# Listing a tile's row maximum and exponential one tile earlier, with a fifth head pair loaded unsplit

## The chip, the cores and the metric

The kernel runs on one core of a Trainium2 chip: TensorE for matrix products and transposes, VectorE, ScalarE and GpSimd for the rest, and DMA queues fed by SyncE. The metric is the device time of one execution in microseconds (us), the median of several. In the profile PE is TensorE (PEld its weight loads), DVE is VectorE, ACT ScalarE, POOL GpSimd, SPq the DMA issues of SyncE.

## What is computed

Attention with a threshold, then a two-layer network, all in float32:

```python
# q, k, v: 8 batches, 8 heads, 576 positions, 64 wide
scores = scale * q @ k.T
thresh = max(scores, -1) - tau
scores = where(scores >= thresh, scores, -1e9)
attn = exp(scores - max(scores, -1))
x = (attn / (sum(attn, -1) + 1e-9)) @ v        # heads side by side: 4608 x 512
h = x @ w_in                                   # 512 x 2048
out = (h * tanh(softplus(h))) @ w_out          # 2048 x 512
```

## The kernel before

Two heads of a batch make a head pair; there are 32 pairs. The 1152 rows of a pair's scores are cut into 9 tiles of 128 rows, so that attention is 288 tiles, and a loop over `g` (line 767) walks through them. Each pass, a step, does one stage of several tiles: scores of tile g+1, the softmax work of g and g-1, the transposes of g-2, the copies of the transposes of g-3, and the products with v some steps later. Batches of the first matrix product (`gemm1`) begin in step 42 and are then fed between the tiles, 14 matmuls in most steps (`advance`, line 858). After the tiles comes the second product.

Every engine but SyncE runs its instructions in the order in which the Python code lists them (class `InOrder`, line 62). So the order of the calls in a step is the order of each engine's queue, and an instruction that waits holds up all behind it on its engine.

The work on one tile:

- `scores` (line 386) multiplies q and k into one of two PSUM buffers `s` (pool `pss`, two buffers of two banks). Pairs 0 to 3 are *plain*: q and k are loaded as float32, and each product is made from the two halves of the array's rows. From pair 4 on each operand is split into a high and a low part after loading, by a ScalarE cast and a GpSimd subtraction for each of its eight pieces (`q_part`, `k_part`).
- `row_max` (line 409), VectorE: the negated maximum of a row of scores, into a small tile `st` (three buffers).
- `exponential` (line 416): the maximum scaled, on ScalarE for tiles below `COLUMNS` and on VectorE from there; the threshold on VectorE; the exponential of the scores on ScalarE, into `e` (two buffers).
- `masked` (line 425): one VectorE instruction compares the scores with the threshold, multiplies by the exponential and adds up each row. It is the last reader of the scores' buffer.
- `total` (line 432): one small instruction that adds 1e-9 to the sum, on ScalarE below `COLUMNS`, on VectorE from there. `normalise` (line 438): a reciprocal on VectorE and a multiplication on GpSimd.
- `transposes` (line 446) on TensorE into `tp` (one buffer); `evacuate` (line 464) copies that out on ScalarE: one copy for an even tile of a pair, two for an odd one, four for the ninth.
- `values` (line 483): a pair's product with v, in two times five pieces that `multiply` takes from a list.

Besides, the steps up to about 57 decode the weights `w_in`, 16 chunks of them. A chunk begun in step n has its `first` (two ScalarE instructions) in step n+3, `clamp` and `shift` (VectorE) in n+4 and n+5, `join` in n+6 (its `sign` on VectorE, its `add` on GpSimd), the cast `upper` (ScalarE) in n+8, and the subtraction `lower` in n+8 on GpSimd or, for the chunks in `ONV`, in n+9 on VectorE. Chunks begin where g mod 18 is 1, 5, 8, 12 or 15.

VectorE's order in a step before the change: row maximum of g, threshold of g, reciprocal of g-1, clamp, shift or lower, sign, mask of g. ScalarE's: copies of tile g-3, total of g-1, scaling of g, exponential of g, `first`, then whatever else the step has. In steps 2 to 37 TensorE has scores of g+1, transposes of g-2 and up to two value pieces; from step 38 (`SOON`) on the transposes come last in the step, and up to five pieces are taken.

Of the kernel before, what the change touches and what calls it, by code (L numbers as in the profile page):

```python
# [16 lines left out]
NP = H // 2  # L17
LOADS = ((0, 0, 2, 4, 5, 4, 7, 6, 7, 8), (0, 3, 3, 2, 5, 4, 5, 8, 8, 9), (0, 1, 2, 6, 3, 4, 7, 5, 7, 8))
# [5 lines left out]
PIECES = 2  # L24
WARM = (24, (26, 12, 6, 4, 3, 2, 2, 2, 2, 2))
SOON = 9 * NP + 2
# [18 lines left out]
SEVEN = range(2, B - 2)  # L45
BEGIN = {42: 0, 78: 1, 9 * 29: B - 2, **{36 * b + 45: b for b in SEVEN}}
MAKE = (66, 5)
COLUMNS = 45
FROM, TO = 36 * SEVEN[0] + 45, 9 * 29
AHEAD = (110, 112, 114)  # L50
XBUFS, TBUFS = 10, 8
# [6 lines left out]
def fv(ap):  # L58
    return ap.bitcast(F32)
# [78 lines left out]
def attention_moe(tc, q, k, v, tau, w_in, w_out, out):  # L138
    nc = tc.nc
    from contextlib import ExitStack  # L140

    with ExitStack() as outer:
# [9 lines left out]
        ident = cst.tile([P, P], F32, name="ident")  # L152
# [97 lines left out]
        nc = Engines(tc)  # L250
        with ExitStack() as first:
# [6 lines left out]
            with ExitStack() as att:  # L258
# [71 lines left out]
                    )  # L330

                def prep(pi):
                    plain = pi < NP
                    qs, k1, k2 = [], [], []
                    for a in range(2):
                        kind = F32 if plain else F32R
                        qs.append(ops.tile([P, 640], kind, name=f"q{a}"))
                        k1.append(ops.tile([P, S + D], kind, name=f"k1{a}"))
                        k2.append(None if plain else ops.tile([P, S + D], kind, name=f"k2{a}"))
                    made = dict(qs=qs, k1=k1, k2=k2, plain=plain)  # L340
                    made["vf"] = ops.tile([P, 2, 5, D], F32, name="vf")

                    def part(src, n):
                        r = raw.tile([P, 320], F32, name="r")
                        nc.sync.dma_start(r[:, :n], src)
                        return r[:, :n]

                    def q_part(c):
                        a, half = divmod(c, 2)
                        sl = slice(half * 320, (half + 1) * 320)  # L350
                        at = slice(c * 320, (c + 1) * 320)
                        if plain:
                            nc.sync.dma_start(qs[a][:, sl], q[pi, :, at])
                            return skip
                        r = part(q[pi, :, at], 320)

                        def split():
                            nc.scalar.copy(qs[a][:, sl], r)
                            nc.gpsimd.tensor_tensor(qs[a][D:, sl], r[D:], fv(qs[a][D:, sl]), ALU.subtract)

                        return split

                    def k_part(a, c):
                        sl = slice(c * 320, (c + 1) * 320)
                        if plain:
                            rows = slice(c * D, (c + 1) * D)
                            nc.sync.dma_start(k1[a][rows, :HB + D], k[pi, rows, a, c * HB:c * HB + HB + D])
                            return skip
                        r = part(k[pi, :, a, sl], 320)

                        def split():
                            nc.scalar.copy(k1[a][:, sl], r)
                            nc.gpsimd.tensor_tensor(k2[a][:, sl], r, fv(k1[a][:, sl]), ALU.subtract)

                        return split

                    def v_part(a):
                        nc.sync.dma_start(made["vf"][:, a], v[pi, :, a])
                        return skip

                    loads = [lambda c=c: q_part(c) for c in range(4)]
                    loads += [lambda a=a, c=c: k_part(a, c) for a in range(2) for c in range(2)]
                    loads += [lambda a=a: v_part(a) for a in range(2)]
                    return made, loads
# [24 lines left out]
                def row_max(s):  # L409
                    st = sm.tile([P, 8], F32, name="st")  # L410
                    e = sm.tile([P, 2, HB], F32, name="e", bufs=2)
                    nm = st[:, 0:1]
                    nc.vector.tensor_reduce(nm, s[:, :, :HB], AX.XY, ALU.max, negate=True)
                    return st, e

                def exponential(g, s, st, e):
                    nm = st[:, 0:1]
                    if g < COLUMNS:
                        nc.scalar.activation(st[:, 2:3], nm, AF.Copy, scale=SCALE)
                    else:  # L420
                        nc.vector.tensor_scalar(st[:, 2:3], nm, SCALE, None, ALU.mult)
                    nc.vector.tensor_scalar(st[:, 1:2], nm, -1.0, back, ALU.mult, ALU.subtract)
                    nc.scalar.activation(e, s[:, :, :HB], AF.Exp, bias=st[:, 2:3], scale=SCALE)
# [8 lines left out]
                def total(g, st):  # L432
                    if g < COLUMNS:
                        nc.scalar.activation(st[:, 4:5], st[:, 3:4], AF.Copy, bias=1e-9)
                    else:
                        nc.vector.tensor_scalar(st[:, 4:5], st[:, 3:4], 1e-9, None, ALU.add)
# [6 lines left out]
                def odd(g):  # L443
                    return g % 9 % 2

                def transposes(g):

                    both = tiles[g]["both"]
                    at = odd(g) * (S + D)
                    tp = pst.tile([P, 4, P], F32, name="tp")  # L450
                    for c in range(4):
                        nc.tensor.transpose(tp[:, c, :], both[:, at + c * P:at + (c + 1) * P], ident)
                    t5 = None
                    last = g % 9 == 8
                    if odd(g) or last:
                        t5 = pst.tile([P, 512], F32, name="t5")[:, :P]
                        if last:
                            nc.tensor.transpose(t5, both[:, S - P:S], ident)
                            nc.tensor.transpose(t5[:D], both[:, S - D:S], ident)
                        else:  # L460
                            nc.tensor.transpose(t5, both[:, 4 * P:5 * P], ident)
                    return tp, t5
# [241 lines left out]
                NT = NPAIRS * 9  # L704
                clock = [0]
# [4 lines left out]
                tiles = {}  # L710
# [7 lines left out]
                def start_pair(g, pi):  # L718
                    parts, todo = prep(pi)
                    pairs[pi] = dict(ops=parts, pt={})  # L720
                    for work, step in zip(todo, LOADS[0 if pi == 1 else 1 if 2 <= pi < NP else 2]):
                        loads.setdefault(g + step, []).append(work)

                def begin(g):
# [12 lines left out]
                def multiply(n):  # L737
                    for _ in range(n):
                        if pieces:
                            work, then = pieces.pop(0)  # L740
                            work()
                            if then:
                                ready.append(then)
# [13 lines left out]
                warm_up(WARM[0])  # L757
                pairs[0] = dict(pt={})
                pairs[0]["ops"], todo = prep(0)
                splits = [todo[i]() for i in FIRST[:3]]  # L760
                nc.sync.dma_start(back, tau)
# [5 lines left out]
                for g in range(NT + 6):  # L767
# [24 lines left out]
                        tiles[g - 2]["tp"] = transposes(g - 2)  # L792
                    done, ready[:] = ready[:], []
                    if not seven:
                        multiply(5 if g >= SOON else PIECES)
                    if g >= NT:
                        done += ready
                        ready.clear()
                    if g < NT:
                        tiles[g]["st"], tiles[g]["e"] = row_max(tiles[g]["s"])  # L800
                    if 1 <= g <= NT:
                        total(g - 1, tiles[g - 1]["st"])
                    if g < NT:
                        exponential(g, tiles[g]["s"], tiles[g]["st"], tiles[g]["e"])
                    for work in now:
                        if len(work) == 2:
# [28 lines left out]
                        chores.setdefault(max(g + 2, 2), []).append(work())  # L835
                    if weights and g % 18 in W1_STEPS:
                        decoding.append([()] * LAG + weights.pop(0)())
                    if g < NT:
                        if g < JOIN:
                            for work in now:  # L840
                                if len(work) == 3:
                                    work[2]()
                        if not odd(g):
                            both = sm.tile([P, S if g % 9 == 8 else 2 * S], F32, name="p" if g % 9 < 8 else "p8", bufs=2 if g % 9 < 8 else 1)
                        tiles[g]["both"] = both
                        half = both[:, S:] if odd(g) else both[:, :S]
                        tiles[g]["p"] = masked(g, tiles[g]["s"], tiles[g]["st"], tiles[g]["e"], half)
# [200 lines left out]
```

## Time and profile before

| | before |
|---|---|
| median of 3 runs | 1313.31 us (1312.69 to 1315.34) |
| profiled execution | 1313.38 us, its span 1311.6 us |
| busy, share of the span | TensorE 97%, VectorE 74%, ScalarE 65%, GpSimd 59% |
| mean granted clock of TensorE | 0.995 |

The span runs from the first to the last instruction of the profiled execution. TensorE's matmuls overlap one another and their ends are modelled, so that its busy time is not time at its peak. The granted clock is the share of 2.4 GHz that the chip gives TensorE; it has two levels, 1.0 (2.4 GHz) and 0.5 (1.2 GHz), and a value between is a mean over a stretch.

### The profile page before, as it was taken

How to read it: one execution, taken by the hardware profiler on the slowest of the kernel's cores; microseconds unless marked ns; L12 is line 12 of the kernel's file. 1: busy time of each engine (PE TensorE's matmuls, PEld its weight loads, DVE VectorE, ACT ScalarE, POOL GpSimd, SP SyncE). 2: the span in 40 equal slices, each digit the busy share in tenths (PEclk: the TensorE clock that was granted, in tenths of full speed). 3: DMA queues.
4: the chain of work that ended last, by engine and by line, in shares of the span. 5: the costliest groups of instructions: out<-in, count | busy, mean ns of one | idle time of the engine just before them, and what ended most of it. 6: DMA issues, size and time to landing. Idle time of an engine off the chain costs nothing. (4 is left out here: it accounts for less than half of the span.)

```text
span 1311.6 us, 28496 instructions
## 1 busy us (share of the span) xinstructions
PE 1272.1 (97%) x9749; PEld 1142.2 (87%) x9749; DVE 969.6 (74%) x2502; ACT 852.9 (65%) x1678; POOL 777.6 (59%) x1073
## 2 busy tenths in 40 slices
PE   8877999999999999999999999999999999999998
PEld 6435899899888888889888898989889999999998
DVE  6887877777778887888888785537985766667664
ACT  5887877777766666676676666664755554555552
POOL 3788887878776686686677676523303333444431
PEclk9998999999999999999999999999999999999999
DMA  6444555777556656566655654215735444344440
GB/s 185 129 128 124 154 160 149 206 215 235 161 162 189 194 163 204 163 184 196 194 169 176 212 157 142 73 50 166 243 116 158 129 134 141 113 145 134 141 130 32
DMA packets 169825, 205.16 MB, mean 156 GB/s; under 512 B 28880, under 2 KB 142544, under 8 KB 165584
## 3 DMA queue, kind: packets, MB, share of 16 engines
q1 hardware_dynamic: 169680, 203.34, 50.9%
q8 instruction: 77, 1.26, 0.4%
q14 instruction: 68, 0.56, 0.1%
HBM read 143.52 MB, written 59.77 MB: 155 GB/s over the span
## 5 line engine op out<-in xcount | busy, mean ns | idle before, releaser
L72 DVE SCALAR_TENSOR_TENSOR p<-s,st,e 128x576 f32<-128x576 f32 x288 | 234.6, 815 | 130.4 <-ACT e L72 128.6
L72 POOL TENSOR_SCALAR p<-p,st 128x576 f32<-128x576 f32 x288 | 243.8, 847 | 98.0 <-DVE st L72 71.9
L72 POOL TENSOR_TENSOR z<-z 128x256 f32<-128x256 f32 x128 | 124.5, 977 | 222.9 <-DVE z L72 214.1
L72 PE MATMUL s<-k,q 128*128 128x288 f32 (+1 forms) x1280 | 232.3, 326 | 19.2 <-DVE p L72 19.0
L72 ACT ACTIVATE e<-s,st 128x576 f32<-128x576 f32 x288 | 215.7, 749 | 42.9 <-DVE st L72 39.8
L72 DVE TENSOR_REDUCE st<-s 128x1 f32<-128x576 f32 x288 | 217.0, 753 | 22.2 <-PE s L72 22.0
L72 DVE TENSOR_TENSOR gl<-z,gh 128x1792 fp32r<-128x1792 f32 (+1 forms) x72 | 141.7, 1969 | 108.1 <-ACT gh L72 108.1
L72 PEld LDWEIGHTS s<-k,q 128*128 128x128 f32 (+1 forms) x1280 | 173.1, 190 | 48.3 <-DVE p L72 38.9
L72 ACT CAST gh<-z 128x1792 fp32r<-128x1792 f32 (+1 forms) x72 | 116.5, 1620 | 149.8 <-issue 81.1
L72 PE MATMUL h<-xh,w1h 128*128 128x288 f32 x704 | 212.4, 302 | 0.6 <-ACT hst L72 0.6
L72 PE MATMUL h<-xl,w1h 128*128 128x288 f32 x704 | 208.5, 296 | 0.0
L72 PE MATMUL h<-xh,w1l 128*128 128x288 f32 x704 | 207.9, 295 | 0.0
L72 PE MATMUL tp<-ident,p 128*128 128x128 f32 x1152 | 176.9, 276 | 8.5 <-POOL p L72 4.2
L72 PEld LDWEIGHTS tp<-ident,p 128*128 128x128 f32 x1152 | 136.8, 141 | 34.9 <-issue 13.5
L72 ACT COPY hi<-tp 128x512 f32<-128x512 f32 (+1 forms) x160 | 87.4, 546 | 90.0 <-PE tp L72 88.4
L72 PE MATMUL o<-gh,sl 128*128 128x256 f32 x512 | 144.5, 282 | 0.0
L72 PE MATMUL o<-gl,sh 128*128 128x256 f32 x512 | 143.8, 281 | 0.0
L72 PE MATMUL o<-gh,sh 128*128 128x256 f32 x512 | 143.5, 280 | 0.0
L72 PE MATMUL y<-hi,vf 128*64 128x320 f32 (+1 forms) x512 | 139.4, 413 | 0.4 <-ACT tk L72 0.4
L72 PE MATMUL y<-lo,vf 128*64 128x320 f32 (+1 forms) x512 | 139.4, 413 | 0.0
L72 PE MATMUL o<-gl,w2h 128*128 128x256 f32 (+1 forms) x448 | 133.3, 298 | 1.3 <-DVE gl L72 1.3
L72 PE MATMUL o<-gh,w2h 128*128 128x256 f32 (+1 forms) x448 | 133.3, 298 | 1.3 <-DVE hst L72 1.3
(77 smaller groups left out, 3174.0 us busy)
## 6 DMA issues: line engine op xcount, KB each, us to landing
z<-hd SPq DMA_DIRECT2D x144, 256.0 KB, 3.1
wt<-sw SPq DMA_DIRECT2D x32, 1024.0 KB, 5.9
r<-q SPq DMA_DIRECT2D x112, 160.0 KB, 2.3
r<-k SPq DMA_DIRECT2D x112, 160.0 KB, 2.5
hd<-hst SPq DMA_DIRECT2D x56, 256.0 KB, 5.9
vf<-v SPq DMA_DIRECT2D x64, 160.0 KB, 3.6
out_t<-c SPq DMA_DIRECT2D x36, 256.0 KB, 2.5
dec<-w_in SPq DMA_DIRECT2D x16, 512.0 KB, 3.8
```

Of the source, the lines that this page charges most:

```text
L72: made = method(*args, **kwargs)
```

## The change

Row maximum and exponential of tiles 1 to 44 are listed in the step before, behind that step's loads and ahead of its sign step and its mask. `COLUMNS` falls from 45 to 27. Pair 4 is made plain, with the loading steps of the plain pairs 2 and 3. In steps 28 to 42 four transposes of the identity stand ahead of the tile's transposes, into the same PSUM tile. The pieces of the products with v that a step takes become 2, 3 and 2 in steps 38, 39 and 40 (5 before), and stay 5 from 41 on.

```diff
-COLUMNS = 45
+COLUMNS = 27
+SOONER = 44
+PLAIN = 5
+WARM_TILES = (28, 43)
+WARM_UPS = 4
...
                 def prep(pi):
-                    plain = pi < NP
+                    plain = pi < PLAIN
...
                     tp = pst.tile([P, 4, P], F32, name="tp")
+                    if WARM_TILES[0] <= clock[0] < WARM_TILES[1]:
+                        for _ in range(WARM_UPS):
+                            nc.tensor.transpose(tp[:, 0, :], ident, ident)
                     for c in range(4):
...
-                    for work, step in zip(todo, LOADS[0 if pi == 1 else 1 if 2 <= pi < NP else 2]):
+                    for work, step in zip(todo, LOADS[0 if pi == 1 else 1 if 2 <= pi < PLAIN else 2]):
...
-                        multiply(5 if g >= SOON else PIECES)
+                        multiply(5 if g > SOON + 2 else 3 if g == SOON + 1 else PIECES)
...
-                    if g < NT:
+                    if g < NT and not 0 < g <= SOONER:
                         tiles[g]["st"], tiles[g]["e"] = row_max(tiles[g]["s"])
                     if 1 <= g <= NT:
                         total(g - 1, tiles[g - 1]["st"])
-                    if g < NT:
+                    if g < NT and not 0 < g <= SOONER:
                         exponential(g, tiles[g]["s"], tiles[g]["st"], tiles[g]["e"])
...
                     if weights and g % 18 in W1_STEPS:
                         decoding.append([()] * LAG + weights.pop(0)())
+                    if g < SOONER:
+                        tiles[g + 1]["st"], tiles[g + 1]["e"] = row_max(tiles[g + 1]["s"])
+                        exponential(g + 1, tiles[g + 1]["s"], tiles[g + 1]["st"], tiles[g + 1]["e"])
                     if g < NT:
                         if g < JOIN:
```

## Rows read from the trace of the kernel before

**Rows 1.** Busy time in three stretches; share of DMA engines and GB/s last.

```profile
76.17:121.44 45.27, 32.06 (x208) 18.43 (x207) 37.42 (x91) 39.15 (x108) 39.19 (x52) 1.00 0.45 134
121.44:134.54 13.10, 12.23 (x76) 11.09 (x77) 8.39 (x22) 8.64 (x23) 9.59 (x14) 0.75 0.37 111
134.54:300.00 165.46, 165.46 (x1282) 148.90 (x1282) 125.25 (x416) 125.19 (x294) 134.85 (x187) 1.00 0.61 178
```

**Rows 2.** Timeline of one tile, all engines: start, duration, engine, instruction, idle before it.

```profile
60.09 0.74 ACT L72 ACTIVATE e<-s,st 128x576 f32<-128x576 f32 x1
...
60.86 0.82 DVE L72 SCALAR_TENSOR_TENSOR p<-s,st,e 128x576 f32<-128x576 f32 x1 [0.40 <-ACT e L72]
61.23 0.59 ACT L72 COPY hi<-tp 128x512 f32<-128x512 f32 x1
...
61.60 0.75 DVE L72 TENSOR_REDUCE st<-s 128x1 f32<-128x576 f32 x1
61.72 0.20 ACT L72 ACTIVATE st<-st 128x1 f32<-128x1 f32 x1
...
61.74 0.76 PE L72 MATMUL s<-k,q 64*128 64x288 f32 x4 [1.20 <-DVE p L72]
62.39 0.20 ACT L72 ACTIVATE st<-st 128x1 f32<-128x1 f32 x1 [0.47 <-DVE st L72]
62.39 0.21 DVE L72 TENSOR_SCALAR st<-st,back 128x1 f32<-128x1 f32 x1
...
62.52 0.15 DVE L72 RECIPROCAL st<-st 128x1 f32<-128x1 f32 x1
...
62.62 0.74 ACT L72 ACTIVATE e<-s,st 128x576 f32<-128x576 f32 x1
```

**Rows 3.** Timeline: first scores, first row maximum, masks of tiles 0, 26 and 41.

```profile
5.99 1.42 PE L72 MATMUL s<-k,q 64*128 64x288 f32 x8
...
6.82 0.76 DVE L72 TENSOR_REDUCE st<-s 128x1 f32<-128x576 f32 x1 [1.75 <-PE s L72]
...
8.62 0.82 DVE L72 SCALAR_TENSOR_TENSOR p<-s,st,e 128x576 f32<-128x576 f32 x1 [0.79 <-ACT e L72]
...
76.16 0.82 DVE L72 SCALAR_TENSOR_TENSOR p<-s,st,e 128x576 f32<-128x576 f32 x1 [0.72 <-ACT e L72]
...
121.44 0.81 DVE L72 SCALAR_TENSOR_TENSOR p<-s,st,e 128x576 f32<-128x576 f32 x1
```

**Rows 4.** Timeline of ScalarE: copies of an odd tile and of a pair's ninth.

```profile
15.47 0.74 ACT L72 ACTIVATE e<-s,st 128x576 f32<-128x576 f32 x1
...
16.12 0.27 ACT L72 COPY tk<-t 128x128 f32<-128x128 f32 x1
...
16.28 0.59 ACT L72 COPY lo<-tp 128x512 f32<-128x512 f32 x1
...
34.89 0.37 ACT L72 COPY hi<-tp 128x256 f32<-128x256 f32 x1 [0.24 <-PE tp L72]
...
35.66 0.21 ACT L72 COPY tk<-t 64x64 f32<-64x64 f32 x1
```

**Rows 5.** VectorE's groups: decoding in tiles 1 to 27, low halves in 1 to 41.

```profile
L72 DVE TENSOR_SCALAR dec<-dec 128x512 f32<-128x512 f32 (+1 forms) x12 | 5.0, 417 | 0.0
...
L72 DVE SCALAR_TENSOR_TENSOR dec<-dec 128x512 uint32<-128x512 uint32 x6 | 4.0, 672 | 0.0
...
L72 DVE TENSOR_TENSOR w1l<-dec,w1h 128x512 fp32r<-128x512 f32 x3 | 2.8, 923 | 0.0
```

**Rows 6.** Timeline: warm-up transposes, scores at the lower clock, two small VectorE instructions.

```profile
1.36 4.46 PEld L72 LDWEIGHTS warm<-ident 128*128 128x128 f32 x24 [1.36 <-POOL ident masks.py:199]
...
7.34 2.82 PEld L72 LDWEIGHTS warm<-ident 128*128 128x128 f32 x26 [0.39 <-issue]
...
22.21 1.30 PE L72 MATMUL s<-k,q 64*128 64x288 f32 x4 [0.78 <-DVE p L72]
...
137.59 0.27 DVE L72 TENSOR_SCALAR st<-st 128x1 f32<-128x1 f32 x2
```

## The prediction

> **What bounds the kernel now.** I read the busy time in stretches first, to learn where a change to the first 45 tiles can matter. From 134.54 us on TensorE is busy for the whole of the stretch at granted clock 1.00 [rows 1]: it sets the end, and what the first 45 tiles gain or lose arrives at the end one for one. Before that no engine is full. From 76.17 to 121.44 us TensorE is busy 32.06 of 45.27 us, ScalarE 39.15, GpSimd 39.19. From 121.44 to 134.54 us the mean granted clock is 0.75, so that about half of it ran at the lower level, 1.2 GHz instead of 2.4.
>
> Then the timeline of one tile, to see which chain sets its length [rows 2]. The row maximum of a tile starts at 61.60 us, just as the mask before it ends. Its scaled copy on ScalarE starts 0.79 us later, the exponential 0.23 us after that, the mask 0.77 us after an exponential starts (60.09 to 60.86), and the next row maximum 0.74 us after the mask (60.86 to 61.60): 0.79 + 0.23 + 0.77 + 0.74 = 2.53 us. That ring of VectorE and ScalarE is the tile. The scores aren't on it: those at 61.74 us start 0.88 us after the mask started (60.86) that freed their buffer, and their reader is more than a tile away.
>
> The masks' starts date the tiles: tile 0 at 8.62, tile 26 at 76.16, tile 41 at 121.44 us [rows 3]. So tiles 1 to 26 took 67.5 us, 2.60 each, near the ring, and tiles 27 to 41 took 45.3 us, 3.02 each: pair 4's and pair 5's splits load ScalarE and GpSimd there.
>
> **The change, part by part.** *The order.* The exponential of g+1 now runs beside the mask of g, so the old ring is cut. But scores have two buffers. Scores g+1 go into the buffer of tile g-1 and wait for mask g-1; row maximum g+1 waits for them; mask g stands behind row maximum g+1 on VectorE, which runs in the order listed. That is a new ring without the exponential. Mask start to scores start is 0.88 us [rows 2]. Scores start to row maximum start is 0.83 us (5.99 to 6.82, [rows 3]). Row maximum to threshold 0.79, threshold to the next VectorE instruction 0.13 (62.39 to 62.52) [rows 2]. Sum 2.63 us, against 2.53: a slack of a whole tile on the scores is spent and the tile is no shorter.
>
> A second ring runs through ScalarE up to tile 26, where ScalarE still makes the total: the reciprocal of g-1 is listed ahead of row maximum g+1 and waits for total g-1, which stands behind exponential g and the copies out of the transposes. From row maximum g: 0.79 + 0.23 to the exponential, 0.65 to the next ScalarE instruction (15.47 to 16.12, [rows 4]), 0.49 for the copy (61.23 to 61.72), 0.25 from total to reciprocal (0.20 and 0.05 for handing over, as between row maximum and scaling), 0.07 for the reciprocal's slot (VectorE starts an instruction about 0.08 before the one ahead ends, 62.39 + 0.21 against 62.52): 2.48 us. An odd tile copies a tail as well, 0.16 more (16.12 to 16.28); the ninth tile of a pair makes four copies, 0.77 us to the start of the last (34.89 to 35.66) and about 0.23 more [rows 4], so 2.99. The larger ring decides: 2.63 in nearly every step, 2.99 in two.
>
> The weight decoding, formerly in the shadow of the exponential, now partly stands on these rings. Its sign step is listed between threshold g+1 and mask g: 0.67 us [rows 5] less 0.07 of that overlap, 0.60 in full. Clamp and shift (0.42, 0.36 after overlap) stand between reciprocal and row maximum: they add 0.20 in an even step (2.48 + 0.36 against 2.63), 0.36 in an odd one, 0.36 on top of 2.99 in a ninth one, and nothing in the step after a sign step, where ScalarE has caught up. By the schedule in the code, steps 1 to 26 are ten at 2.63, four clamps at 2.83, five shifts at 2.99, five signs at 3.23, one sign at 3.58 and one shift at 3.34 (both after a ninth tile): 75.6 us. **Plus 8.1 us** over 67.5.
>
> Scores at the lower clock took 1.30 instead of 0.76 us [rows 6]. They were off the ring; on it each costs 0.54. The trace shows it for the scores at 22.21 us; I take two of them, **plus 1.0** (none: 0; all 26: 14).
>
> *Tiles 27 to 41.* The total moves to VectorE, and the second ring goes. The scale moves too: two small instructions in a row took 0.27 us where one takes 0.20 [rows 6], so 0.07 to 0.08 more on the ring: 2.71. Fifteen tiles: 40.7. Four sign steps at 0.67, 2.7. In steps 32, 35 and 39 VectorE makes a low half of the weights, 0.92 us [rows 5]: total (0.86 us after the mask, 60.86 to 61.72), its 0.20 and the reciprocal end 1.13 us after the mask started, so it overshoots the scores (1.71) by 0.34, and by 0.75 with a shift in step 35: 1.4. The four warm-up transposes cost 0.11 each (26 in 2.82 us of weight loads, [rows 6]); two value pieces beside them bring TensorE to about 3.0 us in some three steps, 0.9 in all (0 to 1.5). The plain pair removes eight ScalarE casts and eight GpSimd subtractions, off the ring now, and issues its ten loads as pairs 1 to 3 do. Sum 45.7: **plus 0.4**. The relief that the fifth plain pair brings is thus eaten by the ring; the bare 40.7 is the lower end, 4.6 less.
>
> *Tiles 42 to 45.* With the value pieces of step 39 spread (three, then two) and the warm-ups ahead, TensorE should enter the first matrix product at full clock. The stretch's TensorE work of 12.23 us at 0.75 is 9.2 to 9.8 us at full clock, and it has 0.87 of idle [rows 1]: 13.1 becomes about 10.9, **minus 2.2** (0 if the clock falls as before, at most 13.1 x 0.25 = 3.3). The row maximum and exponential listed ahead cost nothing here, hidden by the 14 matmuls of a step, which fill TensorE.
>
> On the warm-ups the trace and a page differ. The first 24 warm-up transposes take 4.46 us of weight loads, 0.186 each, and the 26 that come after eight score matmuls 0.108 each [rows 6]: TensorE sped up on little but transposes. The Trainium skill (TensorE: Matmul & The Clock Gate, Part 4: PE-mode transpose) says that transposes don't count as activity in the same way and that the full clock doesn't engage for them. By the row the sum keeps its minus 2.2; by the page it is 0 there, the fourth rival below. The trace speaks against the page.
>
> Sum: 8.1 + 1.0 + 0.4 - 2.2 = plus 7.3 us. The profiled execution took 1313.4 us (span 1311.6 and 1.8 around it), which is the median of the runs: **1320.7 us**.
>
> **The rivals.** *Faster:* the decoding and the copies fall into the wait for the scores. Then 1 to 26 take 26 x 2.63 = 68.4 (+0.9), 27 to 41 take 40.7 (-4.6), and the last stretch gives 2.2: 1307.5. It decides at the sign steps: masks 2.63 apart there and not 3.2. For it speaks that clamp and shift would fit between 1.18 and 1.71 us after the mask if ScalarE were on time; against it, that sign stands behind the row maximum in an in-order queue. Chance 0.10.
>
> *No change:* the middle, clamps and shifts hidden alone (4 x 0.20 + 5 x 0.36 + 0.36 = -3.0), and the last stretch at its end of 3.3 with the warm-ups free (-2.0): 1315.7. Chance 0.12.
>
> *Low clock on the ring:* steps of 2.9 us instead of 2.6 leave TensorE idler, and the lower clock makes them longer yet, 0.54 each. All of 1 to 26: 13 more, 1334. Against it: from 76.17 to 121.44 us TensorE was busy only 71% at granted 1.00 [rows 1]. Chance 0.10.
>
> *Warm-ups without effect:* the fall of the clock at the start of the first product stays, 1322.9. Chance 0.10.
>
> *That the order doesn't take hold* (a row maximum that waits for its statistics buffer, three of which go round): that buffer is given back by the normalisation of g-2, which ends before mask g-1 does, some 1.5 us ahead of the need; I give it no chance of its own.
>
> **How the numbers follow.** The forecast proper has 0.58 (1317 to 1325 by the bounds of its small terms). The range leaves out the faster rival (0.10) and the low clock (0.10): 1312 to 1330. Within 0.2%, 2.6 us, is about what a measurement of this kernel can't tell from no change: faster 0.12 (the faster rival and a little of the middle), the same 0.12, slower 0.76.
>
> **What would show it.** Masks 0 to 26 some 76 us apart instead of 67.5, with row maxima that wait for TensorE (scores), not masks that wait for ScalarE; sign steps 0.6 us longer than their neighbours; ninth-tile steps in which reciprocal and row maximum wait for ScalarE's total; masks 26 to 41 about as far apart as before; granted clock near 1.00 from mask 41 to the scores of tile 46, and 11 us between them. Wrong it would be if scores start well under 0.88 us after the mask, if the row maximum starts under 0.83 us after them, or if the clock stays low for many tiles.

## The result and the profile after

The change makes the kernel slower: 1327.15 us (median of 6 runs, 1326.86 to 1332.67) against 1314.21 us for the kernel before on the same chip, a ratio of 1.0106 (95% interval 1.0086 to 1.0126). The profiled execution took 1326.98 us, its span 1325.2. The forecast was 1320.7: slower, by the ring that was named, but by 7.3 us where about 13 were measured (the rest is taken apart below).

Busy time in the changed kernel, in stretches cut where those of before were cut [rows 1]: mask of tile 0 to mask of tile 26, to mask of tile 41, to the scores of tile 46, and on. Columns after the length: TensorE, its weight loads, VectorE, ScalarE, GpSimd, granted clock, DMA share, GB/s.

```profile
8.61:89.93 81.32, 61.76 (x375) 34.17 (x375) 55.59 (x151) 54.60 (x146) 43.84 (x67) 0.92 0.43 135
89.93:135.96 46.03, 37.45 (x261) 22.27 (x257) 39.59 (x122) 31.58 (x69) 31.09 (x44) 1.00 0.34 106
135.96:147.96 12.00, 10.84 (x82) 8.36 (x81) 9.09 (x30) 7.26 (x16) 9.63 (x14) 1.00 0.41 123
147.96:300.00 152.04, 152.04 (x1179) 137.34 (x1177) 113.79 (x378) 115.14 (x271) 122.51 (x170) 1.00 0.59 171
```

The first stretch grew from 67.5 [rows 3] to 81.3 us, the second from 45.3 to 46.0, the third fell from 13.1 to 12.0 [rows 1]. That is 13.8 + 0.7 - 1.1 = 13.4 of the span's 13.6 us: all of it lies ahead of 147.96 us, and TensorE is full from there on, as before from 134.54. The first stretch alone has a granted clock below 1.00 now.

One tile of the changed kernel on the timeline, to be laid beside [rows 2]:

```profile
14.57 0.81 DVE L76 SCALAR_TENSOR_TENSOR p<-s,st,e 128x576 f32<-128x576 f32 x1
14.67 0.74 ACT L76 ACTIVATE e<-s,st 128x576 f32<-128x576 f32 x1
15.30 0.08 DVE L76 DVE_READ_ACCUMULATOR p<-s,st,e 128x1 f32 x1
15.31 0.58 ACT L76 COPY hi<-tp 128x512 f32<-128x512 f32 x1
...
15.48 0.76 PE L76 MATMUL s<-k,q 64*128 64x288 f32 x4 [0.71 <-issue]
15.78 0.21 ACT L76 ACTIVATE st<-st 128x1 f32<-128x1 f32 x1
16.02 0.16 DVE L76 RECIPROCAL st<-st 128x1 f32<-128x1 f32 x1 [0.64 <-ACT st L76]
...
16.35 0.76 DVE L76 TENSOR_REDUCE st<-s 128x1 f32<-128x576 f32 x1 [0.16 <-PE s L76]
...
17.14 0.21 DVE L76 TENSOR_SCALAR st<-st,back 128x1 f32<-128x1 f32 x1
17.27 0.81 DVE L76 SCALAR_TENSOR_TENSOR p<-s,st,e 128x576 f32<-128x576 f32 x1
```

The rows show the new ring closed: mask at 14.57, scores 0.91 us later at 15.48, row maximum 0.87 after them at 16.35, threshold 0.79 later, next mask 0.13 after that at 17.27. That makes 2.70 us, where the forecast had 2.63 and the old ring 2.53. The exponential at 14.67 does run beside the mask, as the change wants; the next mask doesn't wait for it.

Who waited on VectorE in tiles 1 to 26, first before, then after (total us, times, longest):

```profile
DVE p L72 <- ACT e L72: 10.4, 20, 0.8
```

```profile
DVE st L76 <- ACT st L76: 16.1, 26, 1.1
DVE st L76 <- PE s L76: 8.1, 12, 2.1
```

The masks' wait for the exponential is gone. In its place the reciprocal waits for ScalarE's total in every step and the row maximum for TensorE's scores in twelve.

Two things that the forecast had at too low a price, or not at all, show next: the lower clock and a pair's ninth tile. The four-microsecond windows around tiles 20 to 22, with columns as above:

```profile
64.00:68.00 4.00, 2.38 (x14) 1.41 (x14) 2.80 (x8) 2.72 (x10) 2.49 (x4) 0.82 0.18 67
68.00:72.00 4.00, 3.09 (x14) 1.50 (x11) 2.36 (x8) 2.24 (x7) 2.87 (x4) 0.50 0.08 10
72.00:76.00 4.00, 4.00 (x17) 1.92 (x16) 2.38 (x6) 2.88 (x7) 2.53 (x4) 0.50 0.40 146
76.00:80.00 4.00, 3.99 (x27) 1.88 (x25) 2.57 (x7) 2.03 (x5) 0.72 (x3) 0.90 0.13 45
```

The timeline of the changed kernel inside that stretch and, ahead of it, at a pair's ninth tile:

```profile
25.71 0.81 DVE L76 SCALAR_TENSOR_TENSOR p<-s,st,e 128x576 f32<-128x576 f32 x1
...
26.59 1.24 PE L76 MATMUL s<-k,q 64*128 64x288 f32 x8 [1.38 <-DVE p L76]
...
27.94 0.76 DVE L76 TENSOR_REDUCE st<-s 128x1 f32<-128x576 f32 x1 [0.61 <-PE s L76]
...
73.43 0.81 DVE L76 SCALAR_TENSOR_TENSOR p<-s,st,e 128x576 f32<-128x576 f32 x1
...
74.64 0.74 PE L76 MATMUL y<-hi,vf 128*64 128x320 f32 x1
...
75.31 1.33 PE L76 MATMUL s<-k,q 64*128 64x288 f32 x4
...
76.76 0.76 DVE L76 TENSOR_REDUCE st<-s 128x1 f32<-128x576 f32 x1 [2.08 <-PE s L76]
```

At 1.2 GHz not only the scores are long (1.33 us). The value pieces ahead of them on TensorE's queue are long too, so that the scores start 1.88 us after the mask (73.43 to 75.31) and not 0.88, and the row maximum waits 2.08 us. And the ninth tile of a pair has eight score matmuls, 1.24 us: its row maximum starts 2.23 us after the mask, not 1.71.

### The profile page after: what moved, and what is told of

Read it like the earlier page. It is cut to its first block, busy times and chain, and to the rows that moved or that the text cites. A ratio compares the mean times of both kernels' runs of the same rounds, so it can differ in the third digit from the quotient of the medians.

```text
span 1325.2 us, 28594 instructions
## 1 busy us (share of the span) xinstructions
PE 1281.0 (97%) x9809; PEld 1145.1 (86%) x9809; DVE 972.9 (73%) x2538; ACT 844.6 (64%) x1634; POOL 766.8 (58%) x1065
## 5 line engine op out<-in xcount | busy, mean ns | idle before, releaser
L76 PEld LDWEIGHTS s<-k,q 128*128 128x128 f32 (+1 forms) x1280 | 170.0, 189 | 60.1 <-DVE p L76 48.2
```

Of the source, the lines that this page charges most:

```text
L76: made = method(*args, **kwargs)
```

## The experiments

Times are medians. Each experiment ran beside the kernel before on its own chip, where that took 1314.1 to 1314.5 us; the first row is the run of the profile shown before. The distances between masks are read from the timeline of each run's profile, which is of one execution:

| kernel | time, us | masks 0 to 26 | masks 26 to 41 | masks 41 to 45 |
|---|---|---|---|---|
| before | 1313.3 | 67.5 | 45.3 | 14.7 |
| changed | 1327.2 | 81.3 | 46.0 | 13.5 |
| e1_no_ahead | 1307.4 | 67.2 | 41.1 | 13.0 |
| e2_ahead_alone | 1338.9 | 82.3 | 55.0 | 15.6 |
| e3_sign_first | 1323.6 | 79.6 | 44.6 | 12.9 |
| e4_warm_early | 1325.9 | 80.3 | 46.0 | 13.6 |
| e5_thrice_before | 1315.8 | 68.0 | 48.2 | 13.4 |
| e6_thrice_after | 1327.9 | 82.4 | 46.0 | 13.6 |
| e7_total_vector | 1328.0 | 80.5 | 46.1 | 13.6 |
| e8_repaired | 1321.3 | 77.1 | 44.2 | 12.9 |
| e9_fifth_split | 1309.0 | 69.1 | 43.0 | 12.6 |
| e10_no_warm | 1308.0 | 67.1 | 41.1 | 12.6 |
| e11_pieces_before | 1308.6 | 67.2 | 42.4 | 12.9 |
| e12_old_vector | 1308.9 | 67.0 | 41.0 | 13.0 |

**Is it the order? e1_no_ahead: the change without it.**

```diff
-SOONER = 44
+SOONER = 0
```

> The change without its order: row maximum and exponential of every tile in their own step, all else as changed. If the order makes the ring of mask, scores and row maximum and that ring carries the loss, masks 0 to 26 come back to 67.5 us apart (81.3 with the change), masks 26 to 41 to 40 to 43 us (46.0), and the whole is 3 to 7 us faster than before, 1307 to 1311. Rival: the loss lies in the other parts (total and scale on VectorE, warm-ups on TensorE's queue, the pieces spread): then this stays above 1320.

Measured: 1307.4 us, ratio to before 0.9952 (0.9937 to 0.9967), faster than both kernels. Both distances and the time came as the ring theory had them. The other parts of the change gain some 6 us on the kernel before, and the order takes 19.7 us of the attention's start (masks 0 to 45, 140.9 against 121.2). The version without it is the one to keep.

**e2_ahead_alone: the kernel before with the order only.**

```diff
+SOONER = 44
...
-                    if g < NT:
+                    if g < NT and not 0 < g <= SOONER:
                         tiles[g]["st"], tiles[g]["e"] = row_max(tiles[g]["s"])
...
+                    if g < SOONER:
+                        tiles[g + 1]["st"], tiles[g + 1]["e"] = row_max(tiles[g + 1]["s"])
+                        exponential(g + 1, tiles[g + 1]["s"], tiles[g + 1]["st"], tiles[g + 1]["e"])
```

> The kernel before with the order alone: tiles 1 to 44 ahead, ScalarE's total and scale to tile 44, pair 4 split, no warm-ups in steps 28 to 42, pieces as before. If the order carries the loss: masks 0 to 26 81 us apart as with the whole change, masks 26 to 41 48 to 52 us, since the ring through ScalarE stays and ScalarE has pair 4's casts too, and 1331 to 1337 in all, more than the whole change. Rival (the order costs only the 8 us forecast and other parts the rest): 1318 to 1323.

Measured: 1338.9 us, ratio 1.0183 (1.0166 to 1.0200), above the range expected, since masks 26 to 41 took 55.0 us and not 48 to 52. The clock fell there too, in three places; one window of eight microseconds of the last:

```profile
128.00:136.00 8.00, 5.06 (x22) 3.50 (x21) 6.01 (x16) 4.98 (x16) 5.98 (x10) 0.59 0.34 97
```

The order alone costs more than the whole change. How much of the excess is clock and how much pair 4's casts on the ring through ScalarE, this run doesn't part.

**e3_sign_first: the sign step out of the ring.**

```diff
+                    for work in now:
+                        if len(work) == 3 and g < SOONER:
+                            work[2]()
                     if 1 <= g <= NT:
                         normalise(tiles[g - 1]["st"], tiles[g - 1]["p"])
...
-                        if g < JOIN:
+                        if SOONER <= g < JOIN:
```

> The whole change, with the decoding's sign step and GpSimd's addition behind it listed at the head of the step, ahead of the reciprocal, in steps 0 to 43. If the sign stands on the ring between row maximum and mask, it now falls into the wait for the scores: six times 0.60 and four times 0.67 less, 6 us, 1320 to 1322. Rival: the decoding was never on the path and the loss is clock and scores alone: 1326 to 1328.

Measured: 1323.6 us, 3.6 us under the changed kernel where 6 were expected: masks 0 to 41 gave back 3.1 us. Sign steps did fall to the ring wherever nothing else held them: step 14 from 3.27 to 2.66 us, step 18 from 3.30 to 2.69. But the granted clock fell once more than in the changed kernel, at 24 to 32 us (0.86 and 0.71 in its two windows of four), and steps 7 and 8 took 4.20 and 3.21 us instead of 3.76 and 2.69. So the decoding is on the ring, against the rival; of its price this run gives back a good half. The lower clock took part of the rest, and the ring through ScalarE another part: steps 16 and 19, which come after sign steps, grew from 3.15 to 3.64 and from 2.67 to 2.94 us at full clock, and in step 16 the reciprocal waits for ScalarE's total:

```profile
57.22 0.16 DVE L76 RECIPROCAL st<-st 128x1 f32<-128x1 f32 x1 [1.48 <-ACT st L76]
```

**e4_warm_early: warm-ups from step 4.**

```diff
-WARM_TILES = (28, 43)
+WARM_TILES = (4, 43)
```

> The whole change, with the four warm-up transposes from step 4 on instead of 28. If the fall to the lower clock at 42 to 48 and 66 to 78 us costs steps 13 and 20 to 22 some 3 us and transposes keep the clock up, masks 0 to 26 come to 78 us apart, granted clock 1.00 throughout, 1323 to 1325. Rivals: the transposes don't keep the clock up, and the rows still show 0.5 there, 1327; or they themselves hold up scores on TensorE's queue in every step with value pieces, 1328 to 1332 at full clock.

Measured: 1325.9 us, a gain of about 1 us of the 3 expected. The clock stayed at 1.00 in the windows from 64 to 80 us, and steps 21 and 22 fell from 3.84 and 4.25 to 3.27 and 2.66 us; but it fell once at 44 to 52 us and step 13 grew from 3.91 to 4.68. Half hit: with the transposes the clock held in one place and not in the other. That it held longer is not the chance of one profile: the four runs of this kernel have mean granted clocks of 0.998 to 0.999, the six of the changed kernel 0.987 to 0.996.

**Are the scores on the ring? e5_thrice_before and e6_thrice_after: six tiles' scores made three times over.** The same edit in the kernel before and in the changed one:

```diff
+THRICE = (10, 11, 15, 19, 20, 24)
...
+                        for _ in range(3 if clock[0] in THRICE else 1):
                             for n, (a, col) in enumerate(TURN[t]):
                                 for c in range(2):
```

> The kernel before, with the score matmuls of six tiles (made in steps 10, 11, 15, 19, 20 and 24, which take no value pieces or hardly any) run three times over, each time from zero, so that the scores stay what they were: some 1.1 us more of TensorE in each. In the old order the scores have a tile's slack: those tiles keep 2.54 us and the whole 1312 to 1316. If scores stood on the path there too, 1318 to 1321.

> The whole change with the same six scores run three times over. If mask, scores and row maximum are the ring, steps 15 and 19 go from 2.67 to about 3.7 us in full, the other four by 0.3 to 0.8, since ScalarE's ring or the clamp is already longer there: 4 to 5 us more in these steps, less what the added TensorE work saves by holding the clock up (at most 3). If the scores aren't on the ring, these steps stay as they are, as in the old order.

Measured: 1315.8 us and 1327.9 us, one run each. In the kernel before none of the six steps, nor of those behind them, grew by more than 0.06 us, but for step 11: 3.36 instead of 2.56, where the ninth tile's transposes stood behind the added matmuls, and with them the copies and the total (step 10 was 0.31 shorter). The rest of its added time comes from step 40, 6.39 us instead of 3.40, where the clock fell (0.50 from 112 to 116 us), not from these. In the changed kernel all six grew: step 15 from 2.67 to 3.64, step 19 from 2.67 to 3.64, the others by 0.35 to 0.70, 4.3 us together, as expected. Step 15 of e6 on the timeline:

```profile
51.79 0.81 DVE L77 SCALAR_TENSOR_TENSOR p<-s,st,e 128x576 f32<-128x576 f32 x1
...
52.66 1.73 PE L77 MATMUL s<-k,q 64*128 64x288 f32 x12 [1.13 <-DVE p L77]
...
54.50 0.76 DVE L77 TENSOR_REDUCE st<-s 128x1 f32<-128x576 f32 x1 [1.46 <-PE s L77]
...
55.43 0.81 DVE L77 SCALAR_TENSOR_TENSOR p<-s,st,e 128x576 f32<-128x576 f32 x1
```

In the plain steps 15 and 19 all that is added to the scores (1.73 - 0.76 = 0.97 us) arrives in the next mask; in the other four something else had held the mask already, and less arrives. The run shows a second thing. With six scores made longer the whole is within 1 us of the changed kernel, since the clock stayed up; the windows that answer to those at 0.50 above:

```profile
68.00:72.00 4.00, 2.54 (x19) 1.49 (x16) 2.52 (x8) 2.53 (x9) 1.46 (x3) 1.00 0.00 0
72.00:76.00 4.00, 2.68 (x17) 1.31 (x17) 3.20 (x8) 2.82 (x8) 2.35 (x4) 1.00 0.45 131
```

In the steps that this edit doesn't touch, 12, 13, 21 and 22 took 2.67, 2.94, 3.27 and 2.67 us instead of 2.94, 3.91, 3.84 and 4.25. So the lower clock costs the changed kernel 0.27 + 0.97 + 0.57 + 1.58 = 3.4 us; e4, with the clock up, has the same 3.27 and 2.67 in steps 21 and 22.

**e7_total_vector: total and scale on VectorE throughout.**

```diff
-COLUMNS = 27
+COLUMNS = 0
```

> The whole change with total and scale on VectorE from tile 0. If ScalarE's ring, through the copies and the total, holds up reciprocal, clamp and row maximum to tile 26, then clamp and shift steps fall to the scores' ring: some 3.5 us less, against 26 times 0.07 more for the scale on the ring: 1.5 to 2 us less, 1325 to 1326. Rival: no such ring: 2 us more, 1329.

Measured: 1328.0 us, no gain; masks 0 to 26 took 80.5 instead of 81.3, but the first mask came 1.8 us later in this profile. The steps show the ring through ScalarE gone: shift steps 6, 10, 17 and 24 fell from 2.94 to 2.72 to 2.75 us, while plain steps rose from 2.67 to 2.71 to 2.72 to 2.77. What was won is smaller than what the clock, which fell twice here too, moves from run to run. For the time it stays open; the second ring itself is shown.

**Is the ring the floor? e8_repaired: every other cost removed at once.**

```diff
-COLUMNS = 27
+COLUMNS = 0
-WARM_TILES = (28, 43)
+WARM_TILES = (10, 43)
-WARM = (24, (26, 12, 6, 4, 3, 2, 2, 2, 2, 2))
+WARM = (24, (8, 12, 6, 4, 3, 2, 2, 2, 2, 2))
```

and the edit of e3_sign_first.

> The whole change with all that the runs so far found beside the scores' ring taken away: sign step at the head of the step, total and scale on VectorE throughout, four warm-up transposes from step 10 on, and 8 of them instead of 26 behind the first scores. If the ring itself is the floor, masks 0 to 26 come to 26 x 2.71 and 0.5 for each ninth tile, 72 to 74 us, masks 26 to 41 to 44.6, and the whole to 1316 to 1319: still no better than before and 8 us or more above the old order with the other parts. Rival: the loss was decoding, ScalarE and clock alone: 1307 to 1310.

Measured: 1321.3 us, ratio 1.0047 (1.0030 to 1.0064), 2 us above the range: the clock fell twice near the start, first behind the 8 warm-ups that stand in for 26, then where it also fell in e3 with all 26, in the windows

```profile
8.00:16.00 8.00, 5.94 (x34) 4.50 (x32) 4.53 (x17) 2.83 (x4) 2.10 (x4) 0.79 0.95 274
24.00:32.00 8.00, 6.44 (x27) 3.89 (x27) 5.40 (x20) 2.64 (x6) 3.93 (x5) 0.57 0.13 36
```

From step 9 on the steps lie at the ring, ten of them in steps 9 to 24 at 2.72 to 2.76 us, even with a sign step inside; the other six, at 2.94 to 3.21, have value pieces ahead of the scores on TensorE's queue or, step 16, the ninth tile. Step 12 of this run:

```profile
43.33 0.81 DVE L76 SCALAR_TENSOR_TENSOR p<-s,st,e 128x576 f32<-128x576 f32 x1
...
44.20 0.76 PE L76 MATMUL s<-k,q 64*128 64x288 f32 x4 [0.95 <-DVE p L76]
...
45.07 0.76 DVE L76 TENSOR_REDUCE st<-s 128x1 f32<-128x576 f32 x1 [0.21 <-PE s L76]
...
46.06 0.81 DVE L76 SCALAR_TENSOR_TENSOR p<-s,st,e 128x576 f32<-128x576 f32 x1
```

0.87, 0.87 and 0.99 us make 2.73. With decoding, ScalarE and most of the clock out of the way the order still doesn't reach the 2.54 us of the old one. A third buffer for the scores, which would take their wait for the mask away, was not tried.

**What the other parts are worth: e9_fifth_split, e10_no_warm, e11_pieces_before, e12_old_vector**, each one edit to e1_no_ahead.

```diff
-PLAIN = 5
+PLAIN = 4
```

> The old order with the other parts, but pair 4 split as before. If the fifth plain pair is what frees ScalarE and GpSimd in tiles 27 to 41, masks 26 to 41 go from 41.1 to 44 or 45 us and the whole to 1310 to 1312. Rival: total and scale on VectorE and the spread pieces do it: 1307 to 1308.

Measured: 1309.0 us (median of 7 runs, 1308.1 to 1311.7; the profiled one took 1311.7, and its clock fell at 60 to 72 us). Masks 26 to 41, at full clock, took 43.0 us, less than expected: the plain pair is worth 1.9 of the 4.2 us won in that stretch, and neither theory had it right.

```diff
-WARM_UPS = 4
+WARM_UPS = 0
```

> The old order with the other parts, without the warm-up transposes of steps 28 to 42. If they hold the clock up into the first matrix product, the granted clock falls to 0.5 somewhere from 105 to 125 us, masks 41 to 45 take 14 to 15 us instead of 13.0, and the whole 1309 to 1310. Rival: transposes count for nothing, the clock stays as it was: 1307 to 1308.

Measured: 1308.0 us, the rival's time: the clock didn't fall at the first matrix product, and masks 41 to 45 took 12.6 us. It fell in another place instead, at tiles 29 to 32; the windows there and at the product:

```profile
84.00:92.00 8.00, 6.87 (x35) 3.51 (x37) 7.20 (x26) 5.82 (x11) 5.11 (x8) 0.79 0.13 46
...
112.00:120.00 8.00, 6.29 (x40) 3.66 (x41) 7.32 (x25) 6.76 (x15) 7.70 (x11) 1.00 0.66 201
120.00:128.00 8.00, 7.95 (x64) 6.32 (x62) 6.32 (x19) 5.81 (x13) 7.53 (x11) 1.00 0.45 128
```

```diff
-                        multiply(5 if g > SOON + 2 else 3 if g == SOON + 1 else PIECES)
+                        multiply(5 if g >= SOON else PIECES)
```

> The old order with the other parts, but the value pieces of steps 38 to 40 as before (up to five in step 39). Since the warm-ups turned out not to be needed for it, if the spread pieces are what brings TensorE into the first matrix product without an idle stretch and at full clock, then the clock falls to 0.5 in 105 to 130 us again, masks 38 to 45 take 22.5 us or more instead of 22.0, and the whole 1309 to 1310. Rival: the shorter steps alone do it: 1307 to 1308.

Measured: 1308.6 us. Step 40 took 3.41 us instead of 2.54, and masks 38 to 45 23.3 instead of 22.0: the spread pieces are worth 1.3 us. But the clock stayed at 1.00, so that this half of the expectation fell.

```diff
-COLUMNS = 27
+COLUMNS = 0
```

> The old order with the other parts, and total and scale on VectorE from tile 0, as a possible better version. In the old order the reciprocal that waits for ScalarE lengthens steps 16 and 19 (3.34 and 2.74 us): with the total on VectorE they should fall to 2.55, masks 0 to 26 to 66.2 to 66.6 us (67.2), the whole to 1306 to 1307. Rival: the scale's 0.07 us counts in each step there too: 68 to 69 us, 1309.

Measured: 1308.9 us, no gain. Steps 16 and 19 fell to 3.01 and 2.55 us, but masks 0 to 26 gave only 0.2 us in the profile, in which the clock fell at 60 to 68 us. By its median e1_no_ahead remains the best version of this study, but e10, e11 and e12, run on other chips, lie within 1.5 us of it, and its own runs go from 1307.3 to 1309.9.

## Why the forecast was right and where it was off

**The new ring: right.** Scores 0.88 to 0.91 us after the mask, row maximum 0.83 to 0.87 after the scores, mask 0.92 after that: 2.67 to 2.71 us in the plain steps against 2.63 forecast. e5 and e6 show it directly, e1 takes it away, e8 shows it with most else taken away.

**The ring through ScalarE and the decoding on both: right in kind and size.** Shift steps 2.94 us (forecast 2.99), sign steps 3.27 to 3.30 (3.23), the ninth-tile steps 11 and 20 3.59 and 3.28 (3.58 and 3.34), the steps after a sign step 2.67 to 2.69 (2.63; 2.76 in step 26, where the scale of tile 27 is on VectorE already). Without the clock, the ninth tiles' scores and the first step, tiles 1 to 26 come to 13.8 - 3.4 - 1.4 - 0.6 = 8.4 us more than before; forecast 8.1.

**The step that failed: "Scores at the lower clock ... I take two of them, plus 1.0".** The term was put at 1.0 us, two scores at 0.54; e6 against the changed kernel gives 3.4 us in four steps. Of the 6.1 us by which the sum misses the span (4.7 in masks 0 to 26, 0.3 in 26 to 41, 1.1 behind them) this is the largest single piece, 2.4. The price was wrong as well as the number: at the lower clock the value pieces ahead of the scores on TensorE's queue lengthen too, and step 22 alone lost 1.58 us, three times the 0.54 of its scores.

**Two terms were left out.** The ninth tile's scores are eight matmuls, on the ring in steps 7, 16 and 25: 0.53, 0.32 and 0.52 us, 1.4 together. And in step 1 the scores of tile 2 stand behind the rest of the 26 warm-ups: it took 3.25 us instead of 2.63; e8, with 8 of them, 2.75. With the clock's 2.4 beyond the forecast these make 4.4 of the 4.7 us by which masks 0 to 26 miss the forecast (75.6 + 1.0).

**Tiles 27 to 41: right in the sum, in part by luck.** 46.0 us measured, 45.7 forecast. That the relief there is eaten by the ring is shown by e1, where it comes to light: 41.1. The ring (2.73 us in the plain steps), the sign steps (about 0.60 each) and the value pieces (about 0.8) came near their terms. But the low halves took 0.67 us each, not 0.92, and cost some 0.3 instead of 1.4. About 1.6 us that wasn't in the sum filled the gap: 0.50 for the eight score matmuls of the ninth tile in step 34, 0.65 for a clamp that took 1.32 us in step 37, 0.46 for a sign that took 1.14 us in step 39. Why these two took longer stays open.

```profile
111.71 1.24 PE L76 MATMUL s<-k,q 64*128 64x288 f32 x8 [0.95 <-DVE p L76]
...
121.57 1.32 DVE L76 TENSOR_SCALAR dec<-dec 128x512 f32<-128x512 f32 x1
...
129.23 1.14 DVE L76 SCALAR_TENSOR_TENSOR dec<-dec 128x512 uint32<-128x512 uint32 x1
```

**Tiles 42 to 45: half the gain, and partly for another reason.** The clock stayed at 1.00, but the stretch gave 1.1 us and not 2.2. The forecast had the order at no cost there, and it does cost something: the row maximum of tile 44 waits 1.61 us for eight score matmuls that stand behind the first product on TensorE, and step 43 takes 4.67 us (2.56 in e1):

```profile
141.79 0.76 DVE L76 TENSOR_REDUCE st<-s 128x1 f32<-128x576 f32 x1 [1.61 <-PE s L76]
```

Most of that comes back in step 44 (1.12 us, 3.81 in e1). Without the order, in e1, the stretch takes 11.4 us (117.33 to 128.75), so that the order accounts for some 0.6 of the missing 1.1 us; the other 0.5 was an estimate too low. The warm-ups, which the forecast credited, weren't needed for the clock in the old order (e10), so the clock there was right by luck. What keeps it up there is not shown: neither warm-ups, nor plain pair, nor spread pieces alone brought its fall back.

**The rivals.** The faster one fell at the point it named: sign steps 3.3 us apart. The low clock on the ring was right as a mechanism, in four steps and not in all 26. The fourth, warm-ups without effect, fell in its outcome: the clock didn't fall at the first product. But e10 has it at 1.00 there without warm-ups too, so that this place doesn't decide what transposes do. e4 does: with nothing more than transposes it holds the clock over 64 to 80 us, where the changed kernel fell to 0.50, though it still fell to 0.59 at 44 to 48 us. That e10 falls at 84 to 92 us, where e1 doesn't, rests on one profile each and decides nothing: the mean granted clocks of their runs overlap (0.997 to 0.998 and 0.997 to 0.999). The Trainium skill (TensorE: Matmul & The Clock Gate, Part 4: PE-mode transpose) says that the full clock doesn't engage for transposes. e4 differs from that, and here the runs decide.

## What to carry to other kernels

Before a stage is listed a tile earlier, follow its input's buffer round: with two buffers the work that was ahead by a tile comes onto the path, and what was hidden behind the old wait (decoding, warm-ups, one long tile in nine, a lower clock) is paid. Cutting a ring helps only if the ring that closes in its place, with everything else in its engines' queues, is shorter; add up both from rows of the trace before. In a change of many parts run the parts apart: here four of them together gained 6 us and the fifth lost 20 (25 when alone, e2).

## What the runs showed of the hardware that wasn't expected

Ahead of the first product, where TensorE has idle time, the place at which the granted clock falls moved with small edits. With six longer scores it stayed at 1.00 through tiles 1 to 45 (e6), with four more transposes a step it fell once and not twice (e4), and in the old order it fell at 60 to 72 us (e9), at 60 to 68 (e12), at 84 to 92 (e10) or nowhere ahead of 150 us (e1, e11). Part of this is chance: the seven runs of e9, one kernel, have mean granted clocks from 0.996 to 1.000. In the old order a fall mostly cost little, since the scores are off the ring, but not always: in e9 masks 0 to 26 took 69.1 us instead of 67.2.

Added TensorE work can thus pay for itself: e6 did 6 times 0.97 us more of it, on the path, and its one run took 1327.9 us beside the 1327.2 of the changed kernel.
